# The keys of chunk 7: transposed by the DMA crossbar in place of TensorE

## The chip, the core and the metric

The kernel runs on one NeuronCore of a Trainium2 chip. TensorE (PE) does the matmuls, VectorE (DVE), ScalarE (ACT) and GpSimd (POOL) do elementwise work, and SyncE (SP) issues the transfers, which 16 DMA engines carry out. The metric is the time on the device in microseconds (us), the median of several runs; lower is better.

## The reference, cut to what matters

A retention layer with a decaying state is followed by a feed-forward network (FFN) with a product in the middle. There are 4 batches, 8 heads, 768 tokens and a head size of 64; the model width is 512, the inner width 1024.

```python
for t in range(S):
    state = gamma * state + k[:, :, t] (x) v[:, :, t]     # outer product
    y[:, :, t] = scale * q[:, :, t] @ state
x = y.transpose(0, 2, 1, 3).reshape(3072, 512)
a = x @ w1
b = x @ w2
h = a * b @ w3
out = h @ w_out
```

## The kernel before

**Tiling.** Each batch is cut into 6 chunks of 128 tokens, so that there are 24 chunks (steps), numbered 0 to 23. Inside a chunk the retention is computed as a masked product: scores = keys times queries, times a mask, times values; across chunks a state of 64x64 per head is carried. Heads are taken in pairs, four pairs in all. The FFN takes blocks of 256 tokens (the early ones are narrower). w3 and w_out are multiplied together once at the start, so the FFN is two matmul stages: a and b (`a_unit`, `b_unit`), their product in `HT`, and `o_unit`.

**The order of work** is written out by hand; nothing is rescheduled. Every engine executes its instructions in the order in which the program emits them. The prologue (lines 645 to 797) treats the weights and chunks 0 to 3. From chunk 4 on `step(n)` (line 600) is called once for each chunk. It emits, for n of 4 and above: the casts of chunk n+2 on GpSimd (`casts`, line 333), the scores of chunk n, some FFN units, `kv(n)` (the state), the DMA transposes of chunk n+2, the loads of chunk n+4, more FFN units, `outputs(n)`, `transposes(n+1)`, and the rest of the FFN units. In step 5 `outputs(5)` and `transposes(6)` stand in the middle of an o unit. FFN units come from the queue `fill` and are what PE does between the pieces of the retention.

**Keys.** The scores need the keys of a chunk with the head dimension on the partitions, so they are transposed. The result always ends in `KP[n % 2]` (tile `kp`), which holds the two heads of a pair in two halves padded with zeros; two copies on ScalarE fill it. There are two ways to it:
- By TensorE: `transposes_front` (line 417) makes four transposes, one per head pair, of `k16` (tile `k`, the keys in 16 bits) into a PSUM tile `psT`; `transposes_back` (line 424) copies the upper and lower halves from there (lines 426 and 230, the latter through the helper `cast_to`).
- By DMA: `dma_transposes` (line 385) issues one transpose of `k16` into the SBUF tile `kT` from SyncE (line 391), two steps ahead of its use; `transposes` (line 406) then only makes the two copies from `kT` (lines 411 and 412). `kT` has two buffers.

`by_dma(n)` chooses. With `DT0` = 6 the chunks 0 to 5 and chunk 7 go by TensorE, chunk 6 and chunks 8 to 23 by DMA. Queries of chunk 6 and above always go by DMA, for two chunks at once (tile `qTd`, line 395).

**SyncE's queue.** All loads, stores and DMA transposes are issued from SyncE, in program order. An instruction in it that waits holds everything behind it. A transpose waits for the cast of its chunk on GpSimd, a store of an output for the copy on ScalarE.

**Consumers.** `scores(n)` (line 429) makes eight 128x128 matmuls (line 437), in which `kp` is the stationary operand; the even ones use the half that the first copy filled, the odd ones that of the second. DVE multiplies them by the mask (line 442), and `outputs(n)` (line 472) uses the result.

Of the kernel before, what the change touches and what calls it, by code (L numbers as in the profile page):

```python
# [18 lines left out]
def kernel(  # L19
# [18 lines left out]
    DT0 = 6  # L38
# [341 lines left out]

    def by_dma(n):

        return n >= DT0 and n != DT0 + 1

    def dma_transposes(n):

        if n < DT0 or n >= NSTEP:
            return
        if by_dma(n):
            kT = att.tile([128, NP, 128], HP, tag="kT", name="kT", bufs=2)  # L390
            nc.sync.dma_start_transpose(kT[:, :, :], k16s[n][:, :])
            kTs[n] = kT
        if n % 2 == 0:
            qT = att.tile([128, 2, NP, 128], HP, tag="qTd", name="qTd", bufs=2)
            nc.sync.dma_start_transpose(
                qT[:, :, :, :].rearrange("p t a i -> p (t a) i"), q16s.pop(n // 2)[:, :]
            )
            qTd[n // 2] = qT
# [7 lines left out]
    def transposes(n, tag="psT"):  # L406
        if n >= NSTEP:
            return
        if by_dma(n):
            kT, kp = kTs.pop(n), KP[n % 2]  # L410
            nc.scalar.copy(kp[0:64, :, 0, :], kT[0:64, :, :])  # L411
            nc.scalar.copy(kp[64:128, :, 1, :], kT[64:128, :, :])  # L412
            return
        transposes_front(n, tag)
        transposes_back(n)
# [416 lines left out]
```

## Time and profile before

| what | value |
|---|---|
| time, median of 5 runs | 195.13 us (194.91 to 195.69) |
| the profiled execution, its own time | 194.94 us |
| its span in the profile | 193.0 us |
| granted TensorE clock | 1.00 |
| DMA transposes of keys (`kT`) | 17 |
| transposes of keys on TensorE (line 421) | 28, i.e. four for each of 7 chunks |
| chunk 7: its cast on GpSimd | 57.25 us, 0.61 long |
| chunk 7: its four transposes on the chain | 64.03 us, 0.22 in all |

A profile is one execution. Times in it are microseconds from the start of the span. The chain of waits goes back from the last instruction to whatever released it, so its pieces sum to the span. For a DMA, the length of its line on SyncE's queue is the time that the issue took, and the time to landing counts from the start of the issue until the data has arrived.

### The profile page before, as it was taken

What the parts mean: (1) busy time and instruction counts of PE and PEld (TensorE: products, weight loads), DVE (VectorE), ACT (ScalarE), POOL (GpSimd) and SP (SyncE); (2) the same over time, 40 slices, a digit from 0 to 9 for tenths busy, and PEclk for the clock granted to TensorE, in tenths of its full rate; (3) what the DMA queues carried; (4) which work ended last, traced back from release to release, by engine and by line L of the source; (5) the groups of instructions that cost most, each with busy time, mean ns of one, the idle gap of its engine ahead of it and who ended that gap; (6) DMA issues with size and microseconds to landing.
All of it is one profiled execution on the core that took longest, in us unless ns stands there. A gap on an engine that the chain in (4) does not pass through costs nothing.

```text
span 193.0 us, 4697 instructions
## 1 busy us (share of the span) xinstructions
PE 185.7 (96%) x1777; PEld 140.8 (73%) x1777; DVE 117.2 (61%) x220; ACT 99.5 (52%) x192; POOL 86.2 (45%) x146
## 2 busy tenths in 40 slices
PE   6899999989999999999999999999999999999993
PEld 2345568677797789777877797788777877887752
DVE  3225499599587758656665676565656665753220
ACT  5478575772455464454635463555355545533322
POOL 7600278738872757547153652862425532200000
PEclk9999999999999999999999999999999999999999
DMA  5999999999799999999999999969979931111104
GB/s 197 368 389 395 297 401 322 362 297 208 160 233 207 239 203 237 136 260 226 212 249 233 210 228 217 207 156 270 198 172 194 216 96 20 58 54 54 39 28 155
DMA packets 85030, 40.54 MB, mean 210 GB/s; under 512 B 61328, under 2 KB 80016, under 8 KB 85008
## 3 DMA queue, kind: packets, MB, share of 16 engines
q1 hardware_dynamic: 85008, 40.25, 88.5%
q8 instruction: 14, 0.23, 0.6%
q14 instruction: 8, 0.07, 0.2%
HBM read 29.36 MB, written 6.29 MB: 185 GB/s over the span
## 4 chain that ended last, share of the span: by engine, by line
PE 88%; DVE 7%; DMA 2%; issue 1%; ACT 1%; DVEq 0%
PE psF L508 39%; PE psO L534 21%; PE psA L437 5%; PE psW L280 3%; PE psY L477 3%; PE psY L478 3%; PE psF L724 2%; DMA stg<-in_moe_w_dram 2%; PE psY L480 2%; PE psK L460 2%; DVE am L442 2%; PE psW L293 1%; DVE vp L318 1%; PE psW L259 1%; PE psZ L639 1%
## 5 line engine op out<-in xcount | busy, mean ns | idle before, releaser
L508 PE MATMUL psF<-xt,w 128*128 128x256 f16 (+1 forms) x736 | 85.1, 266 | 0.0
L508 PEld LDWEIGHTS <-w 128*128 128x128 f16 x768 | 68.2, 98 | 7.2
L524 DVE TENSOR_TENSOR ht<-pa,psF 128x256 f16<-128x256 f32 x88 | 36.5, 416 | 23.0 <-PE psF L508 12.7
L518 ACT COPY pa<-psF 128x256 f32<-128x256 f32 x84 | 31.2, 372 | 33.7 <-PE psF L508 33.2
L442 DVE TENSOR_TENSOR am<-psA,keep 128x512 f16<-128x512 f32 x48 | 30.9, 684 | 20.6 <-PE psA L437 20.5
L534 PE MATMUL psO<-w3o,ht 128*128 128x512 f16 x184 | 43.3, 379 | 0.0
L469 POOL TENSOR_TENSOR t<-s,GS 128x512 f16<-128x512 f32 x15 | 19.3, 1284 | 32.0 <-DVE s L468 32.0
L539 ACT ACTIVATE osb<-psO 128x512 f32<-128x512 f32 x23 | 13.7, 597 | 35.1 <-PE psO L534 35.1
L534 PEld LDWEIGHTS <-ht 128*128 128x128 f16 x184 | 17.8, 98 | 16.9 <-DVE ht L773 0.2
L344 POOL TENSOR_TENSOR vp<-v,VS 128x256 f16<-128x256 f32 x40 | 23.8, 615 | 9.5 <-DMA v<-in_v_dram 4.1
L327 POOL CAST q<-q 128x1024 f16<-128x1024 f32 x12 | 13.1, 1093 | 29.8 <-DMA q<-in_q_dram 29.8
L485 DVE TENSOR_TENSOR xt<-psY,YS 128x512 f16<-128x512 f32 x24 | 17.8, 742 | 3.9 <-PE psY L480 3.6
L477 PE MATMUL psY<-am,vp 128*128 128x128 f16 x96 | 16.8, 219 | 0.6 <-ACT kp L230 0.4
L478 PE MATMUL psY<-am,vp 128*128 128x128 f16 x96 | 16.7, 219 | 0.6 <-DVE vp L318 0.6
L437 PEld LDWEIGHTS <-kp 128*128 128x128 f16 x192 | 12.5, 98 | 4.9 <-DVE kp L228 0.4
L340 POOL CAST k<-k 128x512 f16<-128x512 f32 x20 | 12.2, 611 | 5.3 <-DMA v<-in_v_dram 2.2
L468 DVE TENSOR_TENSOR s<-psK,t 128x512 f32<-128x512 f32 x16 | 11.0, 688 | 3.0 <-PE psK L460 2.7
L251 DVE COPY w3t<-psW 128x1024 f16<-128x1024 f16 x8 | 5.4, 688 | 11.3 <-PE psW L259 8.8
L411 ACT COPY kp<-kT 64x512 f16<-64x512 f16 x17 | 10.5, 618 | 2.8 <-DMA kT<-k 2.4
L437 PE MATMUL psA<-qTd,kp 128*128 128x128 f16 x144 | 11.1, 219 | 0.0
L480 PE MATMUL psY<-qTd,t 128*128 128x128 f16 x60 | 10.8, 219 | 0.0
L412 ACT COPY kp<-kT 64x512 f16<-64x512 f16 x17 | 10.5, 615 | 0.4
(82 smaller groups left out, 193.8 us busy)
## 6 DMA issues: line engine op xcount, KB each, us to landing
stg<-in_moe_w_dram SPq DMA_DIRECT2D x16, 512.0 KB, 7.8
q<-in_q_dram SPq DMA_DIRECT2D x12, 512.0 KB, 6.0
out_dram<-osb SPq DMA_DIRECT2D x23, 256.0 KB, 4.0
k<-in_k_dram SPq DMA_DIRECT2D x20, 256.0 KB, 5.2
v<-in_v_dram SPq DMA_DIRECT2D x20, 256.0 KB, 5.5
stg<-in_moe_w_out_dram SPq DMA_DIRECT2D x4, 512.0 KB, 8.0
stg<-in_k_dram SPq DMA_DIRECT2D x2, 512.0 KB, 10.7
stg<-in_v_dram SPq DMA_DIRECT2D x2, 512.0 KB, 8.1
```

The costliest lines, as they stand in the source:

```text
L344: nc.gpsimd.tensor_tensor(vp[:, :, r, r * 64 : r * 64 + 64], v32[:, :].rearrange("j (p s e) -> j p s e", s=2, e=64)[:, :, r, :], VS[:, :]. ...
L437: nc.tensor.matmul(ps[:, i, r, :], lhsT=kp[:, p, r, :], rhs=queries(n, p), start=True, stop=True)
L442: nc.vector.tensor_tensor(am[:, half * 2 : half * 2 + 2, :, :].rearrange("j p s i -> j (p s) i"), ps[:, :, :, :].rearrange("j p s i -> j ( ...
L469: eng.tensor_tensor(t16[:, :, :], s32[:, :, :], GS[:, :, :], MULT)
L477: nc.tensor.matmul(ps[:, p, :], lhsT=vp[:, p, 0, :], rhs=am[:, p, 0, :], start=True, stop=False)
L478: nc.tensor.matmul(ps[:, p, :], lhsT=vp[:, p, 1, :], rhs=am[:, p, 1, :], start=False, stop=(c == 0))
L480: nc.tensor.matmul(ps[:, p, :], lhsT=Tst[0][:, p, :], rhs=queries(n, p), start=False, stop=True)
L485: nc.vector.tensor_tensor(XT[n // 2][:, :, n % 2 * C : (n % 2 + 1) * C].rearrange("p a (i t) -> p a t i", t=2), ps[:, :, :].rearrange(orde ...
L508: nc.tensor.matmul(ps[:, i * w : (i + 1) * w], lhsT=W[d][:, (f + i) * 128 : (f + i + 1) * 128], rhs=XT[self.tok0 // TB][:, d, c0 : c0 + w] ...
L518: nc.scalar.copy(self.pa[f][:, :], ps[:, :])
L524: nc.vector.tensor_tensor(self.HT[:, f : f + TB // self.width, :].rearrange("p f n -> p (f n)"), self.pa.pop(f)[:, :], ps[:, :], MULT,)
L534: nc.tensor.matmul(psO[:, :], lhsT=self.HT[:, f, tb * 128 : (tb + 1) * 128], rhs=W3O[f][:, :], start=(f == 0), stop=(f == 7),)
```

## The change

Chunk 7 is no longer an exception: its keys, too, are transposed by a DMA transpose. The diff is one line:

```diff
     def by_dma(n):
 
-        return n >= DT0 and n != DT0 + 1
+        return n >= DT0
```

By this, PE's four transposes of chunk 7 and the PSUM tile that they fill are gone. ScalarE's two copies into `kp`, at the same two places of its order, now read the SBUF tile `kT` and not PSUM. SyncE's queue gets one more instruction, the DMA transpose of chunk 7, which step 5 emits: it stands behind the loads of q, k and v of chunk 8 (from step 4) and ahead of the loads of k and v of chunk 9. The order of everything else is as it was on every engine; the buffers of `kT` alternate by chunk number from then on.

## The prediction

> **What bounds the kernel now.** I read the page first: engine shares, then the chain that ended last.
>
> ```profile
> span 193.0 us, 4697 instructions
> PE 185.7 (96%) x1777; PEld 140.8 (73%) x1777; DVE 117.2 (61%) x220; ACT 99.5 (52%) x192; POOL 86.2 (45%) x146
> PE 88%; DVE 7%; DMA 2%; issue 1%; ACT 1%; DVEq 0%
> ```
>
> TensorE carries 88% of the chain. A busy PE is not yet a PE at its peak, so I next read the chain in order of time around chunk 7, from 61.94 to 75 us. Columns are start, length, what.
>
> ```profile
> 62.70 0.87 PE psF L508 x8
> ...
> 64.03 0.22 PE psT L421 x4
> 64.25 1.31 PE psF L508 x12
> 65.56 0.58 PE psA L437 x8
> 66.14 1.73 PE psO L534 x8
> ...
> 70.51 1.82 PE psF L508 x16
> 72.33 0.45 PE psA L437 x8
> ```
>
> Here every piece is matmuls, one directly behind the other; the same holds to 190 us. So whatever PE gains or loses at chunk 7 reaches the end in full: no later idle time of PE exists that could swallow it. The first line of interest is L421, the four transposes that the change removes: 0.22 us. The next is L437, the scores of chunk 7: 0.58 us, where the eight matmuls of chunk 8 take 0.45, so 0.13 us of waiting is already in it.
>
> The timeline of ScalarE between 63.9 and 66.3 us and of the weight loads at 65.2 to 66.3 us name that wait:
>
> ```profile
> 64.34 0.58 ACT L426 COPY kp<-psT 64x512 f16<-64x512 f16 x1 [0.35 <-PE psT L421]
> 64.94 0.58 ACT L230 COPY kp<-psT 64x512 f16<-64x512 f16 x1
> 65.57 0.39 PEld L437 LDWEIGHTS <-kp 128*128 128x128 f16 x7 [0.19 <-ACT kp L230]
> ```
>
> Chunk 7's keys are complete in kp at 64.94 + 0.58 = 65.52 us, and seven of the eight weight loads of L437 start at 65.57. This is the point that matters: already now the second copy into kp releases the scores of chunk 7. There is no slack at all.
>
> Last, the timeline of SyncE's queue from 56.9 us (start, duration, what), since the new transpose has to be issued there:
>
> ```profile
> 54.59 2.38 SPq L391 DMA_TRANSPOSE kT<-k  x1
> ...
> 59.68 1.26 SPq L62 DMA_DIRECT2D v<-in_v_dram  x1
> 60.99 1.49 SPq L62 DMA_DIRECT2D k<-in_k_dram  x1
> 62.53 1.09 SPq L62 DMA_DIRECT2D v<-in_v_dram  x1
> 63.71 1.09 SPq L541 DMA_DIRECT2D out_dram<-osb  x1
> 64.90 1.22 SPq L391 DMA_TRANSPOSE kT<-k  x1
> ```
>
> It issues without a pause. The line at 59.68 is v of chunk 8, those at 60.99 and 62.53 are k and v of chunk 9, and the transposes shown are those of chunks 6 and 8. How long kT takes from the start of its issue to its landing, over all 17:
>
> ```profile
> DMA to landing us min/median/max: 2.4/3.6/6.4
> ```
>
> Asked in narrow windows for one issue each, the DMA view gives 4.6 us for chunk 6 (lands 59.19), 5.1 for chunk 8 (70.0), 3.7 for chunk 9, 6.4 for chunk 10, and 2.4 only at 138 us and later, where the queue pauses. Ordinary transfers around the place take as long: v of chunk 8 5.6 us (lands 65.28), k of chunk 9 5.4 (66.39). All landings from 54 to 105 us come in the order of issue.
>
> **What the skill says.** "VectorE: DVE Perf Modes", section "The three transpose paths", puts a 128x128 transpose at 390 ns on TensorE and 1309 ns on the crossbar. The trace agrees in direction for our four blocks (0.22 us of PE's chain against 1.22 us of issue alone), but its landings, 2.4 to 6.4 us, are mostly waiting behind other transfers, and those I use. "DMA: Bandwidth & Descriptors", section "Queues, rings and completion order", says that each DMA engine consumes the descriptors of a ring in order, so a transpose issued behind a load is worked on behind it; the order of the landings agrees. "TensorE: Matmul & The Clock Gate", section "Why this matters for your kernels", warns of PE idle gaps above about 3 us, after which the clock halves; before, no such gap exists after 54 us and the granted clock is 1.00, so the warning is untested here.
>
> **The change, part by part.**
> *Removed.* Four PE transposes, 0.22 us of the chain. Two copies out of psT (0.58 each) become two copies out of kT (0.62 and 0.61): ACT +0.07 us. Both are followed by the same waiting scores.
>
> *Added and moved on SyncE.* One DMA transpose, placed in step 5 between v of chunk 8 and k of chunk 9. It waits for chunk 7's cast on GpSimd, which ended at 57.25 + 0.61 = 57.86 us, so it isn't held; it is issued at 60.99, where k of chunk 9 stands now. Its cost to the queue is 1.22 us by the usual row, up to 2.38 as for chunk 6. Everything behind it moves by 1.2 us at first (bounds 0.5, the smallest gap it could open among the landings, and 2.4): k and v of chunk 9, an output, kT and qTd of chunk 8, q, k, v of chunk 10.
>
> *When it lands.* Lower bound by order: after v of chunk 8, 65.28. A kT lands 0.3 to 0.7 us behind an output store in front of it (0.5 for chunks 8 and 9), and 1.0 behind a v load (chunk 10, the one like case): 65.6 to 66.3. By duration: 60.99 + 4.6 or + 5.1, the two neighbours, 65.6 or 66.1. I take the one of chunk 8, 66.1, since v of chunk 8 in front took 5.6 and k of chunk 9 in the same slot 5.4. Outer bounds are 60.99 + 3.6 = 64.6 (the median) and 60.99 + 6.4 = 67.4.
>
> *The wait it adds.* ACT reaches the first copy at about 64.0 (a pa copy ends at 63.62 + 0.37) and waits there for the DMA. Behind it in ACT's order are the second kp copy and a pa copy at L518, which DVE's ht waits for and behind that the masking of the scores; those three come after the same event and their consumers on PE (next psF bank, outputs of chunk 7) are 1.7 us and more later, so I charge nothing more; without that cover they would cost under 0.8 us (0.37 + 0.41). From landing to the end of the second copy it took 59.87 + 0.61 − 59.19 = 1.29 us for chunk 6 and 70.67 + 0.61 − 70.0 = 1.28 for chunk 8. So kp of chunk 7 is complete at 66.1 + 1.29 = 67.39, against 65.52 before: the scores, and with them the rest of PE's program, start 1.87 us later. The 0.22 us saved on PE is swallowed, because PE merely arrives earlier at a wait.
>
> *What is late next.* kT of chunk 8 would land about 70.0 + 1.2 = 71.2 and its copies end at 72.5; the scores of chunk 8 move to 72.33 + 1.87 = 74.2. Covered by 1.7 us. qTd of chunk 8 (66.17 + 4.7 = 70.9) goes to 72.1, covered as well. v of chunk 9 lands at 68.83 now, 70.0 then; its vp and the state product behind it on POOL end at 71.45 now, 72.7 then, used by outputs at 75.62 + 1.87. Covered. From the output store of 71.03 on SyncE waits for ACT, so it follows PE again.
>
> **Sum.** −0.22 (inside the wait, hence 0) + 1.87 = +1.87 us. The profiled execution itself took 194.94 us (span 193.0 and 1.94 around it): 196.81. It stands 0.19 below the median of 195.13, which gives 197.0 us.
>
> **Rivals.** What a measurement of this kernel can tell from no change is about 0.3%, 0.6 us.
> 1. *Late transpose at chunk 7* (my forecast): kT lands between 65.4 and 66.7, +1.2 to +2.5 us, 196.3 to 197.6. For it: the queue without pause, the landings of neighbours, the order. 70%.
> 2. *Landing half hidden*: kT lands like the median, 64.6 or a little later; kp complete at 65.9, +0.4, to +1.1 at 65.3: 195.5 to 196.2. For it: a kT is only 128 KB by its shape, half of a k load. Against: v of chunk 8 in front lands at 65.28. 12%.
> 3. *Not slower*: the crossbar delivers before PE arrives. PE would arrive at 65.56 − 0.13 − 0.22 ≈ 65.2, so the landing has to come by 65.2 − 1.29 = 63.9, 2.9 us after issue. Then the gain is the 0.22 and the old wait of 0.13, 0.35 us: 194.8. For it: landings of 2.4 to 3.0 late in the run. Against: none below 3.5 before 112 us. It would measure as no change. 6%.
> 4. *Knock-on*: the delayed kT of chunk 8 makes its scores wait too. The cover is 72.33 − 71.28 + 1.87 = 2.9 us; it needs the queue to slip by more, say 4, and then costs 1 us or more: 198.0 to 199. For it: SyncE's back-pressure of up to 2.4 us per issue. Against: one 128 KB transfer opens gaps of about 1 us. A landing as late as 67.4 (+3.2) belongs here as well. 10%.
> 5. *The change doesn't do what it says, or something unseen*: chunk 7 alone changes, one transpose in 17, so only 2% remains for it, either way.
>
> **Numbers.** Likeliest 197.0. The range reaches from the upper part of rival 2 to the lower part of rival 4: 195.8 to 198.2. Slower by over 0.3% means above 195.7: rivals 1 and 4 and most of 2, 0.88. Within 0.3%: the rest of 2 and 3, 0.09. Faster: 0.03.
>
> **What would show it.** Right: an 18th kT at about 61.0 with a landing near 5 us, ACT idle about 2 us before L411 at 66 us on account of DMA, PE with a gap of about 2 us before L437 near 65.2, chunk 8 without a new wait, and everything from chunk 8 on later by the same 1.9 us. Wrong: a kT of chunk 7 issued much before 61 or landing within 3.5 us; a PE gap at chunk 8; or a granted clock below 1.00 after the gap.

## The result, and the profile after

The changed kernel takes 196.14 us (median), the kernel before, run beside it, 195.23. The ratio of the two is 1.003, with a 95% interval of 1.0016 to 1.0043: slower by 0.6 us, 0.3 to 0.8. It compares means, 195.99 and 195.41 us, and leaves out one slow execution of the changed kernel (198.37 us, granted clock 0.991). The forecast was +1.87. The direction holds; the size is a third of what was forecast.

The page of the changed kernel's profile begins so:

```profile
span 193.9 us, 4692 instructions
PE 185.4 (96%) x1773; PEld 140.5 (72%) x1773; DVE 116.8 (60%) x220; ACT 99.6 (51%) x192; POOL 85.8 (44%) x146
PE 72%; DMA 14%; POOL 4%; SPq 3%; DVE 3%; issue 1%; ACT 1%; POOLq 0%; DVEq 0%; ACTq 0%
```

Four matmuls fewer on PE, 0.9 us more of span, and the chain that ended last no longer goes back along PE all the way: 14% of it is now DMA and 3% SyncE's queue. Its course in order of time (start, length, what) shows where it turns off:

```profile
60.55 4.71 DMA kT<-k
65.25 0.02 issue
...
65.33 0.63 ACT kp L411
65.96 0.01 issue
65.97 0.62 ACT kp L412
66.60 0.05 issue
66.64 0.56 PE psA L437 x7
67.21 1.73 PE psO L534 x8
```

The transpose of chunk 7 lands at 65.26, both copies follow it, and the scores of chunk 7 follow the second copy. The weight loads of PE say the same (in brackets the idle time ahead and who ended it):

```profile
66.00 0.10 PEld L437 LDWEIGHTS <-kp 128*128 128x128 f16 x1 [0.77 <-ACT kp L411]
66.64 0.39 PEld L437 LDWEIGHTS <-kp 128*128 128x128 f16 x7 [0.54 <-ACT kp L412]
```

Seven weight loads started at 65.57 before and at 66.64 now. The queue of SyncE in the changed kernel:

```profile
54.59 1.29 SPq L391 DMA_TRANSPOSE kT<-k  x1
...
58.87 1.58 SPq L62 DMA_DIRECT2D v<-in_v_dram  x1
60.55 2.13 SPq L391 DMA_TRANSPOSE kT<-k  x1
62.72 0.58 SPq L62 DMA_DIRECT2D k<-in_k_dram  x1
63.34 0.58 SPq L62 DMA_DIRECT2D v<-in_v_dram  x1
...
64.93 1.22 SPq L391 DMA_TRANSPOSE kT<-k  x1
```

Two things differ from what was forecast. The transpose of chunk 6 took 1.29 us to issue, not 2.38, and v of chunk 8 was issued 0.81 us sooner than in the profile before. And the transpose of chunk 8, the last line, was issued at 64.93, as before (64.90). The new transpose took 2.13 us, but k and v of chunk 9 behind it took 1.16 in place of 2.58. From the first issue behind v of chunk 8 to the transpose of chunk 8 it took 3.9 us before (60.99 to 64.90) and 4.4 after (60.55 to 64.93). In the other profiles it is 3.9 without an extra transfer there, and 4.6 to 4.9 with one: it costs the queue 0.5 to 1.0 us, and here the earlier start hid that.

**How the executions are compared below.** The start of the program differs from execution to execution: the scores of chunk 6, ahead of everything that the change touches, start at 60.4 to 62.2 us, and at 65.3 us in no_transpose7. So I measure from that start (called S6): when v of chunk 8 and kT of chunks 7 and 8 land, when the scores of chunks 7 and 8 end on PE, and how long it is to the end of the span. All are read from the timelines of PE and SyncE and from the DMA view, which gives landings to 0.1 us. The part from the end of the scores of chunk 8 to the end of the span is 120.1 to 120.3 us in all kernels here except the one where chunk 9 waits; so what matters is decided between chunk 6 and chunk 8.

S6 is in us from the start of the span, the columns to its right in us from S6; v8 is v of chunk 8, kT7 the transposed keys of chunk 7.

| profile | S6 | v8 lands | kT7 lands | scores 7 end | kT8 lands | scores 8 end | S6 to end |
|---|---|---|---|---|---|---|---|
| before | 60.56 | 4.7 | | 5.58 | 9.4 | 12.21 | 132.4 |
| before_2 | 62.18 | 4.2 | | 5.59 | 8.5 | 12.15 | 132.4 |
| after | 60.74 | 3.9 | 4.5 | 6.46 | 9.4 | 13.03 | 133.2 |
| after_2 | 60.86 | 3.1 | 3.7 | 5.62 | 8.4 | 12.19 | 132.3 |
| after_3 | 60.44 | 3.8 | 4.2 | 6.24 | 9.1 | 12.80 | 133.0 |
| after_4 | 61.01 | 4.2 | 4.7 | 6.69 | 9.4 | 13.26 | 133.5 |
| no_transpose7 | 65.31 | 2.2 | | 5.33 | 7.1 | 11.89 | 132.1 |
| no_transpose7_2 | 60.61 | 5.0 | | 5.35 | 9.7 | 12.45 | 132.7 |
| spare_transpose7 | 62.23 | 3.8 | 4.4 | 5.59 | 9.2 | 12.14 | 132.4 |
| kt7_first | 61.03 | 5.3 | −0.3 | 5.33 | 9.9 | 12.58 | 132.8 |
| kt7_last | 60.81 | 3.5 | 7.7 | 9.68 | 8.7 | 17.93 | 138.1 |
| kt7_first_k9_late | 60.62 | 5.3 | −0.3 | 5.33 | 8.0 | 11.89 | 134.2 |
| kt7_first_k8_pe | 60.77 | 5.3 | −0.3 | 5.33 | | 12.61 | 132.8 |
| kt7_first_pa_first | 60.50 | 6.0 | 0.2 | 5.33 | 10.6 | 12.44 | 132.7 |

### The profile page after: what moved, and what is told of

The parts are those of the page before. It is cut to its first block, busy times and chain, and to the rows that moved or that the text cites. A ratio compares the mean times of both kernels' runs of the same rounds, so it can differ in the third digit from the quotient of the medians.

```text
span 193.9 us, 4692 instructions
## 1 busy us (share of the span) xinstructions
PE 185.4 (96%) x1773; PEld 140.5 (72%) x1773; DVE 116.8 (60%) x220; ACT 99.6 (51%) x192; POOL 85.8 (44%) x146
## 4 chain that ended last, share of the span: by engine, by line
PE 72%; DMA 14%; POOL 4%; SPq 3%; DVE 3%; issue 1%; ACT 1%; POOLq 0%; DVEq 0%; ACTq 0%
PE psF L508 34%; PE psO L534 18%; DMA stg<-in_v_dram 5%; DMA v<-in_v_dram 4%; PE psA L437 4%; DMA kT<-k 2%; PE psW L280 2%; SPq L62 2%; DMA stg<-in_moe_w_dram 2%; PE psY L478 2%; PE psY L477 2%; POOL vp L318 2%; PE psY L480 2%; PE psK L460 2%; PE psF L724 1%
## 5 line engine op out<-in xcount | busy, mean ns | idle before, releaser
L518 ACT COPY pa<-psF 128x256 f32<-128x256 f32 x84 | 31.3, 372 | 33.8 <-PE psF L508 33.3
L411 ACT COPY kp<-kT 64x512 f16<-64x512 f16 x18 | 11.1, 618 | 2.7 <-DMA kT<-k 2.3
L412 ACT COPY kp<-kT 64x512 f16<-64x512 f16 x18 | 11.1, 615 | 0.4
```

The costliest lines, as they stand in the source:

```text
L518: nc.scalar.copy(self.pa[f][:, :], ps[:, :])
```

## The experiments

Theory A says that the loss is the wait of chunk 7's scores for kT, whose landing is set by its place in a queue that is full. Rival B puts it on something else in the change, rival C on the added transfer as such.

**Chunk 7 without a transpose** (no_transpose7 and no_transpose7_2).

The diffs from here on are cut to what matters and stand against the changed kernel, that of spare_transpose7 against the kernel before.

```diff
-            kT = att.tile(...)
-            nc.sync.dma_start_transpose(kT[:, :, :], k16s[n][:, :])
-            kTs[n] = kT
+            if n != DT0 + 1:
+                kT = att.tile(...)
+                nc.sync.dma_start_transpose(kT[:, :, :], k16s[n][:, :])
+                kT_last[0] = kT
+            kTs[n] = kT_last[0]
```

> Chunk 7's keys are not transposed at all: its two copies read the transposed keys of chunk 6, which landed long before, so that part of the computation is left out. Neither PE's four transposes nor an extra DMA are there. Theory A (the loss is the wait for kT of chunk 7 at its scores, nothing else): the wait is gone, and what is left is the gain of 0.2 to 0.4 us, ratio to before 0.998 (0.997 to 1.000), no PE gap ahead of the scores of chunk 7. Rival B (the loss comes from something else that the change shifts, such as the copies now reading SBUF or the changed buffers of kT): the loss of 0.3% stays, ratio about 1.003.

> As no_transpose7 (chunk 7's transpose left out, its copies read chunk 6's), for a profile with the full granted clock. Theory A: from the scores of chunk 6 to the end of those of chunk 7 5.3 us (5.58 before), to the start of those of chunk 8 11.3 (11.60), and from the scores of chunk 6 to the end of the span 132.1 us (132.4 before). Rival B: 6.2 us or more at chunk 7, as in the changed kernel.

Measured: median 195.46 us, ratio 1.0018 (1.0002 to 1.0034): no gain, though a gain was expected. At chunk 7 theory A is borne out: the scores end at 5.33 and 5.35, 0.24 us sooner than before, and the wait is gone. So copies that read SBUF cost nothing there, and B falls as far as this kernel tests it. It keeps the old alternation of kT's buffers; but in the changed kernel the copies of chunk 6 had left the buffer that chunk 8 now takes at 60.4 us, and its transpose was issued at 64.93, so nothing waited for that either.

The two profiles differ at chunk 8. The first is of the longest execution, 199.66 us. Its granted clock fell ahead of S6, so that PE came to S6 4.7 us later than in the second, and the transfers were well ahead of it (PE busy, granted clock, DMA share, GB/s):

```profile
40.00:48.00 8.00, 6.39 (x47) 0.57 0.88 225
```

It keeps the gain to the end (132.1), but is no fair sample of where the transfers stand. In the second, at a clock of 1.00, the gain turns into a loss of 0.3 us at chunk 8, which I had not expected. ScalarE's timeline of that second profile (the edit shifts line numbers by 3: L414 and L415 are the copies L411 and L412, L521 is L518), and the matmuls of PE that follow:

```profile
70.33 0.62 ACT L414 COPY kp<-kT 64x512 f16<-64x512 f16 x1 [0.70 <-DMA kT<-k]
70.95 0.61 ACT L415 COPY kp<-kT 64x512 f16<-64x512 f16 x1
71.59 0.65 ACT L521 COPY pa<-psF 128x256 f32<-128x256 f32 x2
```

```profile
72.02 0.60 PE L511 MATMUL psF<-xt,w 128*128 128x256 f16 x4 [0.39 <-ACT pa L521]
```

ACT comes 0.70 us too early for the keys of chunk 8. Behind its two copies stands a pa copy (it takes the result of an `a_unit` out of PSUM), which frees the PSUM bank that PE's fourth FFN unit needs; PE waits for that, not for the keys. So the next place that the same queue limits lies one chunk on, with hardly any slack. Where the transfers were well ahead of PE (the first profile, kT of chunk 8 at 7.1) it did not show. The 0.3 us of the second profile is as much as the timed ratio says (0.35 us), but it is one profile.

**The transfer alone** (spare_transpose7): the kernel before, with an extra transpose that nobody reads.

```diff
+        if n == DT0 + 1:
+            spare = att.tile([128, NP, 128], HP, tag="kTs", name="kTs", bufs=1)
+            nc.sync.dma_start_transpose(spare[:, :, :], k16s[n][:, :])
```

> The kernel before, with chunk 7's keys still transposed on PE, and beside it the DMA transpose of chunk 7 issued at the place where the changed kernel has it, into a tile that nobody reads. Theory A: the transfer alone costs nothing, ratio 1.000 (0.999 to 1.001); it lands 4 to 6 us after its issue, the transfers behind it land some 0.5 us later, and the scores of chunk 7 start as before at about 65.5 us. Rival C (the added transfer delays the loads and transposes of chunks 8 and 9, and these cost the time): the loss of the change is here too, ratio 1.003 or more, with a gap at chunk 8 or 9.

Measured: 195.42 us, ratio 1.0012 (0.9992 to 1.0033), which doesn't tell theory A from C by itself. The profile does, for its execution: scores of chunk 7 at 5.59, of chunk 8 at 12.14, 132.4 to the end, each as before. The transfer lands at 4.4, where the changed kernel's four land at 3.7 to 4.7, and delays nothing that counts here. The interval is too wide to say that it never does.

**The transpose earlier** (kt7_first): ahead of the loads of q, k and v of chunk 8.

```diff
         dma_transposes(n + 2)
-        load_chunk(n + 4)
+        if n == 5:
+            load_chunk(8)
+        if n != 4:
+            load_chunk(n + 4)
```

> The changed kernel, with the loads of q, k and v of chunk 8 moved from step 4 to step 5, behind the DMA transpose of chunk 7; the transpose so stands three issues earlier in SyncE's queue. Theory A: it is issued at about 57.9 us, when its cast ends, lands at about 62, before ACT comes for it at 64, and the loss turns into a gain of 0.2 to 0.4 us, ratio 0.998. The loads of chunk 8 land 0.5 to 1.3 us later, which the 1.05 us of slack at the scores of chunk 8 may cover just so; if not, up to 0.5 us come back, ratio 1.000. Rival C: the ratio stays at 1.003 or gets worse, since the same transfer still delays the loads of chunk 8.

Measured: 196.03 us, ratio 1.0033 (1.0007 to 1.0059). Again chunk 7 does what theory A says (kT lands 0.3 us before S6, scores end at 5.33), and chunk 8 takes it back:

```profile
70.87 0.62 ACT L411 COPY kp<-kT 64x512 f16<-64x512 f16 x1 [0.85 <-DMA kT<-k]
71.51 0.62 ACT L412 COPY kp<-kT 64x512 f16<-64x512 f16 x1
72.15 0.65 ACT L518 COPY pa<-psF 128x256 f32<-128x256 f32 x2
```

```profile
72.57 0.60 PE L508 MATMUL psF<-xt,w 128*128 128x256 f16 x4 [0.54 <-ACT pa L518]
```

The loads of chunk 8 are later, hence its casts, its transpose (landing at 9.9) and, through ACT's order, PE. The ratio is as rival C expected, and in this order its reason holds for the loads of chunk 8, which stand behind the transpose now. But it is not the loss of the changed kernel: that one is at chunk 7, and none is left there.

**The transpose later** (kt7_last): behind k and v of chunk 9.

```diff
+        if n == 5:
+            load_chunk(9)
         dma_transposes(n + 2)
-        load_chunk(n + 4)
+        if n != 5:
+            load_chunk(n + 4)
```

> The changed kernel, with the DMA transpose of chunk 7 moved behind the loads of k and v of chunk 9, two issues later. Theory A: it is issued 1.2 to 2.6 us later and lands behind these 512 KB, at 67.3 to 68.5 where it landed at 65.3; the scores of chunk 7 start later by the same amount, so this costs another 2.0 to 3.0 us over the changed kernel, ratio 1.013 to 1.019. Rival C: no further loss, ratio about 1.003, since the number of transfers is the same and those of chunk 9 come earlier.

Measured: six executions of 197.5 to 203.2 us, median 201.12, which is 3.1% above the kernel before beside them. The ratio of 1.019 (1.012 to 1.025) rests on the two shortest alone, so the size is unclear; that it is slower is not. kT lands at 7.7, 3.2 us later than in the first profile of the changed kernel, and the scores of chunk 7 end 3.2 us later: one for one. Then a second loss comes, which was not expected. ScalarE's wait, PE's wait and the o unit behind it, and the engines between 70 and 74 us (busy us by engine, granted clock, DMA share, GB/s):

```profile
68.62 0.62 ACT L411 COPY kp<-kT 64x512 f16<-64x512 f16 x1 [4.39 <-DMA kT<-k]
```

```profile
69.29 0.23 PE L437 MATMUL psA<-qTd,kp 128*128 128x128 f16 x1 [3.71 <-ACT kp L411]
...
70.33 3.29 PE L534 MATMUL psO<-w3o,ht 128*128 128x512 f16 x8
```

```profile
70.00:74.00 4.00, 4.00 (x18) 1.85 (x19) 1.62 (x3) 0.61 (x2) 0.00 (x0) 0.58 1.03 230
```

After 3.7 us without matmuls the granted clock of PE is 0.58 on the mean of these 4 us (0.50 from 71 to 74 us), and eight matmuls take 3.29 us that take 1.89 in the changed kernel, read in the same view. From the end of the scores of chunk 7 to those of chunk 8 it takes 8.25 us, 6.57 in the changed kernel: 1.7 us, of which the o unit alone has 1.4. The warning of the Trainium skill, "TensorE: Matmul & The Clock Gate", section "Why this matters for your kernels", against gaps above about 3 us, agrees with this. But 3 us is no safe limit in this case: in the first profile of no_transpose7 the clock fell to 0.50, for over 6 us from 40.9 us on, in a gap of 1.8 us behind a stretch of shorter ones:

```profile
41.14 0.29 PE L480 MATMUL psY<-am,vp 128*128 128x128 f16 x1 [1.80 <-POOL vp L319]
```

The changed kernel's own gaps at chunk 7, 0.5 and 0.4 us on PE, left it at 1.00.

**Making room for chunk 8** (kt7_first_k9_late): as kt7_first, and k and v of chunk 9 behind the transposes of chunk 8.

```diff
         dma_transposes(n + 2)
-        load_chunk(n + 4)
+        if n in (5, 6):
+            load_chunk(n + 3)
+        if n not in (4, 5):
+            load_chunk(n + 4)
```

> As kt7_first (the transpose of chunk 7 ahead of the loads of chunk 8), and in addition the loads of k and v of chunk 9 moved from step 5 to step 6, behind the two transposes of chunk 8. In kt7_first chunk 7 was 0.25 us quicker than before, but chunk 8 0.6 us slower: its transposed keys landed at 70.9 us, ACT stood 0.85 us at L411, and a pa copy behind it held a PSUM bank that PE needed. Theory A2 (both losses are places in one queue): with the 512 KB of chunk 9 out of its way, kT of chunk 8 lands at about 68, neither chunk waits, and from the scores of chunk 6 to those of chunk 8 it takes 11.3 us, against 11.60 before and 12.42 with the change; ratio 0.998 to 0.999. Rival C (the crossbar transfer itself, or a third wait, costs the time): it stays above 11.6 us and the ratio above 1.001.

Measured: 197.19 us, ratio 1.009 (1.007 to 1.011). Up to chunk 8 it went as theory A2 said: kT of chunk 8 lands at 8.0, its scores start at 71.90 − 60.62 = 11.28 and end at 11.89, 0.3 us ahead of before. But chunk 9 was overlooked. SyncE's queue, and ScalarE:

```profile
68.86 0.57 SPq L62 DMA_DIRECT2D k<-in_k_dram  x1
...
73.78 1.85 SPq L541 DMA_DIRECT2D out_dram<-osb  x1
75.76 1.22 SPq L391 DMA_TRANSPOSE kT<-k  x1
```

```profile
79.32 0.62 ACT L411 COPY kp<-kT 64x512 f16<-64x512 f16 x1 [4.00 <-DMA kT<-k]
```

k of chunk 9 is issued at 68.86, lands 3.5 us later, its transpose gets its turn at 75.76 only, behind a store and the loads of chunk 10, and ACT waits 4 us for it. The loss was moved, not removed.

**More profiles of both kernels** (after_2, after_3, before_2). Theory D says that the size of the forecast came from one profile whose transfers were late.

> The changed kernel once more, for a second profile of it. Theory D (the forecast was too high because the profile before had the transfers of chunk 8 late in relation to PE, by chance): v of chunk 8 lands 3.5 to 4.2 us after the scores of chunk 6 start, where the profile before had 4.7, and the scores of chunk 7 end 6.1 to 6.6 us after that start (5.58 before). Rival E (the landing is always as in the profile before, and the crossbar transfer is quicker than its neighbours): v of chunk 8 lands 4.6 to 4.8 us after it.

> As after_2, a third profile of the changed kernel: under theory D the end of the scores of chunk 7 follows the landing of kT of chunk 7 with a constant distance (1.9 us), from execution to execution, whatever the landing is; under rival E both are the same in every execution to 0.1 us.

> The kernel before once more, for a second profile. Theory D: v of chunk 8 lands 3.5 to 4.2 us after the scores of chunk 6 start, not 4.7 as in the first profile, and the scores of chunk 7 end 5.6 us after it all the same. Rival E: 4.6 to 4.8 again.

Measured: v of chunk 8 lands at 3.1 and 3.8 in the changed kernel, 4.2 in the kernel before. Rival E falls. D's own ranges held in part: before_2 lies at the edge, so 4.7 was late, but not out of the ordinary (no_transpose7_2 has 5.0), and after_2 lies below, with a landing at 3.1 and the scores of chunk 7 at 5.62, not 6.1 to 6.6. It took 195.22 us and has hardly a loss, which its ScalarE shows:

```profile
64.61 0.62 ACT L411 COPY kp<-kT 64x512 f16<-64x512 f16 x1 [0.33 <-DMA kT<-k]
```

What goes with an early or a late landing shows ahead of everything that the experiments change, at the issue of chunk 6's DMA transpose. It took 2.2 to 2.4 us in three profiles (before, no_transpose7_2, kt7_first_pa_first) and 1.3 to 1.4 in all others. One of each, kt7_first_pa_first and before_2:

```profile
54.60 2.24 SPq L391 DMA_TRANSPOSE kT<-k  x1
```

```profile
55.19 1.40 SPq L391 DMA_TRANSPOSE kT<-k  x1
```

In these three v of chunk 8 lands late: at 4.7 and 5.0, against 3.1 to 4.2, where it stands ahead of the transpose of chunk 7 or there is none (no_transpose7 with its late PE left aside), and at 6.0, against 5.3, where it stands behind it. The long issue comes with and without a DMA transpose of chunk 7. What makes it long was not tried.

From the landing of kT of chunk 7 to the end of the scores it takes 1.9 to 2.0 us in the four profiles of the changed kernel and in kt7_last, as near as landings can be read.

**Chunk 8 as the exception** (kt7_first_k8_pe), with the changed kernel once more beside it (after_4). The edit of kt7_first, which it contains, is left out of the diff.

```diff
-        return n >= DT0
+        return n >= DT0 and n != DT0 + 2
```

> As kt7_first, but chunk 8 in place of chunk 7 is the exception that TensorE transposes; so as many DMA transposes as in the kernel before, 17. Theory A2 (what counts is whether a transpose lands ahead of ACT's copies in a queue that is full until about chunk 9; a transpose on TensorE never waits for that queue): chunk 7 is 0.25 us quicker than before, chunk 8 pays 0.22 us for its four transposes and no wait, so from the scores of chunk 6 to those of chunk 8 it takes 11.4 to 11.7 us (11.60 and 11.54 before, 11.97 in kt7_first), and no chunk after waits; ratio 0.999 to 1.001. Rival F (moving the loads of chunk 8 back costs by itself, through its casts or queries): 11.9 us or more and a ratio above 1.002.

> The changed kernel beside the others on one chip, with a fourth profile. Theory D: the end of the scores of chunk 7 comes 1.9 to 2.0 us after the landing of its kT or, where that lands earlier than 3.6 us after the scores of chunk 6 start, 5.3 us after that start; ratio to before 1.000 to 1.004, with executions between no loss at all and 1 us or more.

Measured: kt7_first_k8_pe 195.46 us, ratio 1.0024 (1.0009 to 1.0039); after_4 195.87 us, ratio 1.0034 (1.0021 to 1.0047), which repeats the result. after_4's profile has kT at 4.7 and the scores' end at 6.69, as D says. kt7_first_k8_pe missed its expectation: the scores of chunk 8 start at 72.77 − 60.77 = 12.00, not at 11.4 to 11.7.

```profile
70.72 0.58 ACT L426 COPY kp<-psT 64x512 f16<-64x512 f16 x1 [0.96 <-PE psT L421]
71.31 0.58 ACT L230 COPY kp<-psT 64x512 f16<-64x512 f16 x1
71.92 0.65 ACT L518 COPY pa<-psF 128x256 f32<-128x256 f32 x2
```

These are rival F's numbers, but the trace doesn't show F's reason, the loads: the keys of chunk 8 had been cast at 65.7 us. ACT waits for PE's four transposes, which stand behind the outputs of chunk 7 and start right after them, at 70.30, and the pa copy behind the two kp copies is late again. At chunk 7 three FFN units stand between there and the scores, at chunk 8 four, and the fourth needs a bank that ACT has to free.

**The pa copy first** (kt7_first_pa_first). Again the edit of kt7_first is left out of the diff.

```diff
+        if n == 7:
+            fill.pull(share * 0.125, ready)
         if n not in (4, 5):
             transposes(n + 1)
-        fill.pull(share * 0.5, ready)
+        fill.pull(share * (0.375 if n == 7 else 0.5), ready)
```

> As kt7_first, and in step 7 the first FFN unit ahead of ACT's two copies for chunk 8, so that one pa copy of ACT goes ahead of them; PE's and SyncE's orders stay. Theory G (at chunk 8 PE is held not by the keys but by the pa copy behind ACT's waiting kp copies, which keeps a PSUM bank from PE's fourth FFN unit): PE then reaches the scores of chunk 8 without a wait and the copies end in time or 0.2 us late, so from the scores of chunk 6 to those of chunk 8 it takes 11.3 to 11.5 us (11.97 in kt7_first, 11.60 and 11.54 before), from the scores of chunk 6 to the end 132.1 to 132.3 (132.44 before, 132.77 in kt7_first), ratio 0.998 to 1.000: as fast as before or a little faster. Rival H (the keys of chunk 8 themselves are late for its scores): the same 11.9 us as in kt7_first, ratio 1.003.

Measured: 195.84 us, ratio 1.0029 (1.0009 to 1.0049). PE's wait for the bank is gone and it reaches the scores of chunk 8 at 72.04 − 60.50 = 11.54, but there it now waits for the keys themselves:

```profile
72.01 0.10 PEld L437 LDWEIGHTS <-kp 128*128 128x128 f16 x1 [0.35 <-ACT kp L411]
72.37 0.39 PEld L437 LDWEIGHTS <-kp 128*128 128x128 f16 x7 [0.27 <-ACT kp L412]
```

kT of chunk 8 landed at 10.6 in this execution, later than anywhere else here. G and H are both right in part: the bank was one gate, the landing is the next one behind it. How it goes with a landing at the 9.9 of kt7_first wasn't seen. No version was found that beats the kernel before.

## Why the prediction was right in direction and wrong in size

- *The mechanism* held. Chunk 7's scores have no slack, PE's transposes are replaced by a wait for kT, the 0.22 us saved vanishes in it, and everything after is later by the same amount (about 120.2 us from the scores of chunk 8 to the end, before and after). Undoing the wait alone, or moving it three issues up or two down, moved chunk 7 accordingly. From the landing to the end of the scores the forecast had 1.9 us (5.58 + 1.87 − 5.54), and the runs have 1.9 to 2.0.
- *The step that failed* is "When it lands", the 66.1 us, which is 66.1 − 60.56 = 5.5 after S6. The four profiles of the changed kernel have 4.5, 3.7, 4.2 and 4.7, 4.3 on the mean, 1.2 sooner. Of that, 0.9 is the transfer ahead: v of chunk 8 landed at 4.7 in the one profile that I had, at 3.9, 3.1, 3.8 and 4.2 (mean 3.8) in those four. Another 0.3 is the step from v to kT, 0.45 to 0.6 us, for which I had taken 0.8. With 4.3 the same sum gives 4.3 + 1.96 − 5.58 = +0.7 us, and the profiles average +0.56 from S6 to the end (133.16, 132.34, 132.96, 133.49, against 132.43): what the timed runs say. So the likeliest time should have been that of rival 2, "landing half hidden", to which I gave 12%.
- *Why v of chunk 8 landed late in that profile* is known in part. About half of the 0.9 goes with the execution (4.7 against the 4.2 of before_2, and a long issue of chunk 6's transpose, which comes with and without a DMA transpose of chunk 7). Whether the change itself brings these transfers forward can't be told from two profiles of the kernel before, 4.7 and 4.2, against 3.1 to 4.2 in the changed kernel.
- *Moved by 1.2 us* lay within its bounds of 0.5 to 2.4, but measured from S6 it doesn't show. From the landing of v of chunk 8 to that of kT of chunk 8 it takes 5.2 to 5.5 us in the four profiles of the changed kernel, 4.7 and 4.3 in the two of the kernel before: some 0.8 us more. Since v itself landed sooner, kT of chunk 8 landed at 9.4, 8.4, 9.1 and 9.4, against 9.4 and 8.5 before. That the new issue took over part of a wait that the two loads behind it had anyway is my reading of their shorter issues, not tested.
- *"Whatever PE gains or loses at chunk 7 reaches the end in full"* holds for the loss only. A gain there meets the next gate: I counted 1.05 us of slack to the scores of chunk 8, but a pa copy behind the kp copies holds PE, and in the profile before chunk 8 was already at that edge (its four units took 1.82 us, 1.75 in the changed kernel). It didn't decide the forecast, but it is why taking the wait away gained nothing that stayed.
- *Rival 4*, a knock-on at chunk 8, didn't come in the changed kernel. A wait at chunk 8 did come in each profile in which chunk 7 was relieved and kT of chunk 8 landed at 9.7 or later, but there because PE was earlier or the loads of chunk 8 had been moved back.

## What to carry to other kernels

When a wait is put on a transfer, its price is the landing minus the time of need, and both move from one execution to the next; take the landing from several profiles, each measured from an event just ahead of the place, before trusting a difference of two numbers from one profile. They give the spread more than the right value: the second profile of the kernel before would have lowered this forecast by 0.2 us only, but would have shown that half a microsecond of it was chance. In a queue that is full, moving one transfer up makes another one late: follow the queue until it first runs empty before claiming a gain. And look behind the waiting instruction on its engine: here the copy that held PE was not the one that waited.

## What was not expected of the hardware

- One more transfer in SyncE's full queue cost the issues behind it less than its own issue took: 2.13 us for the transpose in the first profile of the changed kernel, but 1.16 in place of 2.58 for the two loads after it. Over the five profiles that have it there, the stretch up to the transpose of chunk 8 grew from 3.9 us to 4.4 to 4.9.
- The crossbar transpose itself, 128x512 in 16 bits, took 0.45 to 0.6 us of the stream of landings behind a load of 256 KB in the four profiles of the changed kernel, and 2.4 us from issue to landing where the queue ahead had paused for a cast (kt7_first).
